# Powers of minus one half on ScalarE, one K copy by DMA, four more key tiles on VectorE

## The chip, the cores and the metric

The kernel runs on one core of one Trainium2 chip. It has five engines with a queue of instructions each: TensorE (PE, with its weight loads shown as PEld), VectorE (DVE), ScalarE (ACT), GpSimd (POOL) and SyncE (SP), which only issues DMAs here. Each engine takes its instructions strictly in the order in which the program lists them; where one waits on a semaphore, all behind it on that engine wait too. The metric is the device time of one execution in microseconds (us), median of several runs.

## The reference

The program is one transformer layer over 2048 tokens of 448 features, with weights and activations in bf16:

```python
x  = A_x
h  = x + attention(layernorm(x)) @ wo       # 16 query heads of 28, one shared key head and one shared value head
h2 = h + B(layernorm(h))
def B(x):                                   # mixture of depths
    r   = x @ w_r                           # one router score per token
    idx = argsort(-r)[:8]                   # the 8 best tokens
    y   = ((silu(x[idx] @ w_gate)) * (x[idx] @ w_up)) @ w_down
    return x + scatter_add(idx, y * sigmoid(r[idx]))
```

The layernorm is (x - mean) / sqrt(var + 1e-5), so each row of each of the two layernorms needs one power of minus one half. The attention is a full softmax, 16 heads times 2048 by 2048 scores; that is where the time goes.

## The kernel before, in words

**Tiles.** The 2048 tokens are 16 tiles of 128. A query block `b` is one such tile with all 16 heads, which lie as 4 strips of 4 heads; a strip has 32 rows of TensorE (28 features, one row that holds a constant, and padding) and 512 columns (4 heads by 128 queries). For each block and each key tile `j` the kernel makes 4 score products of 128 keys by 512 queries (line 834), turns them into exponentials, and multiplies these with the values of tile `j` (line 863), summed over all 16 key tiles in PSUM bank 7. One of the 32 value columns is a constant, so that the sum of exponentials comes out with the product.

**Two ways to an exponential.** There are 256 pairs of block and key tile. Most are done by ScalarE (`act_tile`, lines 872 to 897): two units of two strips each, 128 x 1024, one Exp per unit (line 888). The others are done by VectorE and GpSimd (`dve_tile`, lines 901 to 941): VectorE clamps the scaled scores of one strip to 16-bit integers, whose bits read as bf16 are a rough power of two (line 909, four per tile); GpSimd adds a constant to all four at once, twice, with a 64-bit integer add (line 920); the three versions are multiplied with three differently weighted copies of the values and so average out the roughness. A tile on VectorE therefore has 12 value products where a tile on ScalarE has 4. `_ND` lists how many of the 16 key tiles VectorE takes in each block: 83 in all, so ScalarE has 173 tiles, or 346 units.

**Two versions of K.** A score product of ScalarE's units is one over 64 rows of TensorE, in which the strip's neighbour is cancelled by zeros in K. So K is stored twice: version 0 has its data in rows 0 to 31 and 64 to 95 and zeros elsewhere, version 1 the other way round (`K[:, i % 2, ...]`, line 834). Both are written by VectorE out of the same PSUM bank (line 787), with per-partition factors in `kcol` that are zero where the version is to be zero. A unit of ScalarE has strips (0, 2), which read version 0, or (1, 3), which read version 1; the first comes first.

**The order of the work.** All instructions are first put into a graph with their dependencies, a planned duration and a priority (`G.op`). A planner (`_Flow.plan`) then walks through planned time, and at each step lists, on the engine that is free first, the ready instruction with the best priority; the result is the fixed order of each queue. Constants such as `_W`, `_LOOK`, `_WIN`, `_LATE` and `_HOLD` shift its choices; a DMA takes part with an issue of 400 ns on SP and a planned latency (`lat`, 2000 ns by default). An instruction with `lock=True` is planned so that it does not lie beside any instruction of GpSimd.

**Before the first block.** The tokens are normalized in groups of tiles (`group`, lines 725 to 800): 0, 1, (2, 3), (4, 5), (6, 7), (8 to 11), (12 to 15). For each: statistics (lines 730, 732), the power of minus one half, the normalized rows (lines 752 to 763), transposes on TensorE, the copy out of PSUM (line 777), the K product and its two writes (line 787), the V product and its write (line 796). In groups 0 to 2 the power is Exp(-0.5 Ln(var + eps)) on ScalarE (lines 735 and 737). From group 3 on it is `rsqrt` on VectorE (lines 713 to 723): a bit trick as first guess and three steps of Newton, with 14 small instructions per group in all. The groups 3 to 6 are worked through during block 0, since its key tiles need them one after the other. The large weights of the second half are loaded by SP at the same time (`weights`, lines 1040 to 1049): each piece of `wg_sb`, `wu_sb` and `wo_pad` waits on SP for an earlier piece to land.

**After each block.** The sum goes from PSUM to `Ot` (line 947), the softmax sums make a round trip through DRAM to be spread over the partitions (lines 951 to 955, four DMAs on SP), VectorE multiplies (`On`, line 956), TensorE projects and adds the residual, and VectorE works out the second layernorm and the router's score for the tile (`out_proj`, lines 962 to 1011): statistics (984, 985), `rsqrt` in its form with one product per step (986, 714 to 723, 8 instructions after line 986), `st3` (989), the router's product with its sum (993), the score `r_col` (996) and the output rows (1008). Block 15 has its own form on a short path (`last_rows`, lines 1013 to 1035), which uses Ln and Exp on ScalarE already.

**The end.** `stage1` (lines 1070 to 1106) finds the 8 best of tiles 0 to 13, gathers their rows and prepares them; `tail` (lines 1108 to 1246) finishes block 15, chooses the 8 best of all and runs the small network on them.

Of the kernel before, what the change touches and what calls it, by code (L numbers as in the profile page):

```python
# [237 lines left out]
MAGIC = 1597463007.0  # L238
# [269 lines left out]
def _fast(nc, G, sb, ps, psb, flag, scr, rows, A_x, A_wq, A_wk, A_wv, A_wo, B_w_r, B_w_gate, B_w_up, B_w_down, out):  # L508
# [178 lines left out]
    for r in range(2):  # L687
# [23 lines left out]
    kv_last = []  # L711

    def rsqrt(y, v, z, a, rd, wr, tmp, one=False):
        G.op(DV, lambda e: e.tensor_scalar(z.bitcast(I32), v.bitcast(I32), -0.5, MAGIC, ALU.mult, ALU.add), 62,
             reads=[rd], writes=[tmp])
        for n, c in enumerate((3.0, 12.0, 768.0)):
            if one:
                G.op(DV, lambda e: e.tensor_scalar(a, z, z, v, ALU.mult, ALU.mult), 62, reads=[tmp, rd], writes=[tmp])  # L718
            else:
                G.op(DV, lambda e: e.tensor_tensor(a, z, z, ALU.mult), 62, reads=[tmp], writes=[tmp])  # L720
                G.op(DV, lambda e: e.tensor_tensor(a, a, v, ALU.mult), 62, reads=[tmp, rd], writes=[tmp])
            G.op(DV, lambda e, c=c: e.scalar_tensor_tensor(z, a, -c, z, ALU.add, ALU.mult), 62, reads=[tmp], writes=[tmp])  # L722
        G.op(DV, lambda e: e.tensor_scalar(y, z, -1.0 / 8192.0, None, ALU.mult), 62, reads=[tmp], writes=[wr])

    def group(g):
# [3 lines left out]
        for t in tl_:  # L729
            G.op(DV, lambda e, t=t: e.bn_stats(bn6[:, t, :], x_sb[:, t, :]), 516, reads=[("x", t)], writes=[("bn6", t)],  # L730
                 after=[G.last_w[("xnT", 0)][0]] if t == 2 else [G.last_w[("nb", 3)][0]] if t in (4, 5) else (), prio=-3001 if g == 2 else None)
# [2 lines left out]
        if g < XA:
            G.op(AC, lambda e: e.activation(var[:, t0:t1], mv[:, t0:t1, 1], ACT.Ln, bias=ebias[:, 0:1]), 200,
                 reads=[("mv", t) for t in tl_] + ["ebias"], writes=[("var", g)])
            G.op(AC, lambda e: e.activation(rstd[:, t0:t1], var[:, t0:t1], ACT.Exp, scale=-0.5), 200, reads=[("var", g)],
                 writes=[("rstd", g)])
        else:
            G.op(DV, lambda e: e.tensor_scalar(var[:, t0:t1], mv[:, t0:t1, 1], EPS, None, ALU.add), 62,  # L740
                 reads=[("mv", t) for t in tl_], writes=[("var", g)])
            G.op(DV, lambda e: e.tensor_scalar(nmu[:, t0:t1], mv[:, t0:t1, 0], -1.0, None, ALU.mult), 62,
                 reads=[("mv", t) for t in tl_], writes=[("nmu", g)])
            rsqrt(rstd[:, t0:t1], var[:, t0:t1], nwt[:, t0:t1], nwt[:, NT + t0:NT + t1], ("var", g), ("rstd", g), ("nwt", g))
            G.op(DV, lambda e: e.tensor_tensor(nb[:, t0:t1], nmu[:, t0:t1], rstd[:, t0:t1], ALU.mult), 62,
                 reads=[("rstd", g), ("nmu", g)], writes=[("nb", t) for t in tl_])
        if 0 < g < XA:
# [38 lines left out]
        for r in range(2):  # L786
            G.op(DV, lambda e, r=r: e.tensor_scalar(K[:, r, sl], ps[:, uk.b[0], 0:w], kcol[:, r:r + 1],
                                                        kcol[:, 2 + r:3 + r], ALU.mult, ALU.add), 190 + w * 1.04,
                     reads=[uk.key, "k%d" % r, "kb%d" % r], writes=[("K", r, t) for t in tl_], free=uk)
# [87 lines left out]
    def spill(end):  # L877
        while strips:
            n = _UNIT[iu[0] % len(_UNIT)]
            if len(strips) < n or (end and len(strips) == 4 and n == 3):  # L880
                if not end:
# [7 lines left out]
                                                           scale=OCT), 63.3 + 426.5 * n,  # L889
# [55 lines left out]
    def evict(b):  # L945
# [11 lines left out]
                                           ALU.mult), 597, reads=[("Ot", rb), ("Rb", rb)], writes=[("On", rb)])  # L957
# [4 lines left out]
    def out_proj(t):  # L962
# [23 lines left out]
        G.op(DV, lambda e: e.tensor_scalar(st[:, t, 0:1], stf[:, 1:2], EPS, None, ALU.add), 62, reads=[("stf", t)],  # L986
# [833 lines left out]
```

## Time and profile before

| | |
|---|---|
| median of 3 runs | 378.29 us (378.02 to 378.76) |
| profiled execution, its own time | 377.05 us |
| span of the profiled execution, first to last instruction | 375.3 us |
| busy: PE, DVE, ACT, POOL | 336.3, 344.7, 335.5, 183.4 us |
| mean granted clock of TensorE | 0.964 of full speed |

A row of a group has the line, the engine, the operation, output and inputs with their shapes, the number of instructions, their busy time together in us, the mean of one in ns, and after the second bar the idle time of the engine just before them with what ended it. Busy time is the union of the instructions' times: where neighbours overlap it is less than number times mean. A row of the timeline has the start in us, the time in us of one or of several merged instructions, and in brackets the idle time before. L624 is the helper that makes a matmul and L636 the one that makes a DMA; there the tiles' names tell which one it is.

### The profile page before, as it was taken

How to read it: one execution, taken by the hardware profiler on the slowest of the kernel's cores; microseconds unless marked ns; L12 is line 12 of the kernel's file. 1: busy time of each engine (PE TensorE's matmuls, PEld its weight loads, DVE VectorE, ACT ScalarE, POOL GpSimd, SP SyncE). 2: the span in 40 equal slices, each digit the busy share in tenths (PEclk: the TensorE clock that was granted, in tenths of full speed). 3: DMA queues.
4: the chain of work that ended last, by engine and by line, in shares of the span. 5: the costliest groups of instructions: out<-in, count | busy, mean ns of one | idle time of the engine just before them, and what ended most of it. 6: DMA issues, size and time to landing. Idle time of an engine off the chain costs nothing.

```text
span 375.3 us, 8937 instructions
## 1 busy us (share of the span) xinstructions
PE 336.3 (90%) x3658; PEld 113.1 (30%) x3658; DVE 344.7 (92%) x859; ACT 335.5 (89%) x377; POOL 183.4 (49%) x197
## 2 busy tenths in 40 slices
PE   3967899999999999999988999999999999998965
PEld 2533332323232323222232323233232322222334
DVE  7999797999999999998989999999989999989884
ACT  5736999999999999989998999999999999998850
POOL 6010165754474647546445357655545656465311
PEclk9989999999999999977999999999999999998995
DMA  6662001001010001010010101010101610100010
GB/s 183 179 223 61 1 3 31 3 12 46 21 37 28 30 4 55 2 52 6 3 56 6 52 2 55 4 55 1 29 30 29 198 39 23 29 30 31 26 36 8
DMA packets 17975, 16.10 MB, mean 43 GB/s; under 512 B 6302, under 2 KB 15038, under 8 KB 17930
## 3 DMA queue, kind: packets, MB, share of 16 engines
q1 hardware_dynamic: 16426, 14.93, 12.8%
q8 instruction: 29, 0.48, 0.5%
q10 hardware_dynamic: 1392, 0.45, 0.5%
q14 instruction: 16, 0.13, 0.1%
q0 software_dynamic: 112, 0.12, 0.1%
HBM read 11.78 MB, written 3.71 MB: 41 GB/s over the span
## 4 chain that ended last, share of the span: by engine, by line
DVE 61%; PE 18%; ACT 11%; DMA 7%; issue 1%; POOL 0%; POOLq 0%; DVEq 0%
DVE Y L909 32%; ACT P L888 11%; PE ps L834 8%; PE ps L624 5%; PE ps L863 4%; DVE st L722 3%; DVE On L956 3%; DMA Rb<-l_scr 3%; DVE st L718 2%; DVE junk L993 2%; DVE of L1008 2%; DVE bn L984 2%; DMA l_scr<-Rc 2%; DMA x_sb<-in_A_x_dram 2%; DVE Ot L947 2%; DVE bn L730 1%
## 5 line engine op out<-in xcount | busy, mean ns | idle before, releaser
L888 ACT ACTIVATE P<-ps 128x1024 bf16<-128x1024 f32 x346 | 323.7, 1064 | 20.4 <-PE ps L834 18.6
L920 POOL INT64_ADD Yc<-Y x166 | 172.9, 1053 | 155.1 <-DVE Y L909 131.8
L909 DVE TENSOR_SCALAR Y<-ps 128x512 int16<-128x512 f32 x332 | 212.7, 679 | 13.0 <-PE ps L834 12.3
L834 PE MATMUL ps<-Q,K 32*128 32x512 bf16 (+1 forms) x1024 | 164.1, 395 | 13.2 <-DVE Y L909 5.0
L834 PEld LDWEIGHTS ps<-Q,K 32*128 32x128 bf16 (+1 forms) x1024 | 42.8, 92 | 142.6 <-ACT P L888 81.8
L863 PE MATMUL ps<-P,Vs 128*32 128x512 bf16 x692 | 65.0, 387 | 2.6 <-ACT P L888 2.2
L863 PE MATMUL ps<-Yc,Vs 128*32 128x512 bf16 x664 | 65.5, 396 | 0.5
L863 PE MATMUL ps<-Y,Vs 128*32 128x512 bf16 x332 | 33.9, 398 | 3.6 <-DVE Y L909 2.0
L863 PEld LDWEIGHTS ps<-Yc,Vs 128*32 128x32 bf16 x664 | 16.4, 94 | 29.4 <-issue 18.1
L863 PEld LDWEIGHTS ps<-P,Vs 128*32 128x32 bf16 x692 | 16.2, 95 | 21.8 <-issue 15.8
L624 PE MATMUL ps<-xnT,wqx 112*128 112x128 bf16 x256 | 21.1, 227 | 0.3 <-DVE Y L909 0.2
L624 PE MATMUL ps<-wo_pad,On 128*32 128x448 bf16 (+1 forms) x244 | 18.3, 357 | 1.6 <-DVE On L1124 1.4
L624 PEld LDWEIGHTS ps<-xnT,wqx 112*128 112x128 bf16 x256 | 15.2, 101 | 8.4 <-issue 5.8
L956 DVE TENSOR_TENSOR On<-Ot,Rb 128x512 bf16<-128x512 f32 x15 | 14.2, 944 | 2.0 <-DMA Rb<-l_scr 2.0
L863 PEld LDWEIGHTS ps<-Y,Vs 128*32 128x32 bf16 x332 | 8.6, 94 | 20.5 <-issue 8.8
L722 DVE SCALAR_TENSOR_TENSOR st<-st 128x1 f32<-128x1 f32 x45 | 13.2, 293 | 0.9
L772 PE MATMUL ps<-ident,of 128*112 128x128 bf16 x64 | 6.7, 259 | 8.0 <-DVE of L752 5.5
L718 DVE TENSOR_SCALAR st<-st 128x1 f32<-128x1 f32 x45 | 11.9, 265 | 0.4
L624 PE MATMUL ps<-x_sb,ident 128*32 128x448 bf16 (+1 forms) x82 | 10.4, 360 | 1.5 <-DVE On L956 1.0
L817 DVE TENSOR_SCALAR Q<-ps,qone 128x512 bf16<-128x512 f32 (+1 forms) x16 | 11.6, 723 | 0.0
L1008 DVE TENSOR_SCALAR of<-ps,st 128x448 bf16<-128x448 f32 x14 | 10.3, 735 | 0.0
L984 DVE BATCH_NORM_STATS2 bn<-ps 128x6 f32<-128x448 f32 x15 | 9.3, 623 | 0.9 <-PE ps L624 0.9
(170 smaller groups left out, 172.7 us busy)
## 6 DMA issues: line engine op xcount, KB each, us to landing
Rb<-l_scr SPq DMA_DIRECT2D x15, 256.0 KB
out_dram<-of SPq DMA_DIRECT2D x16, 112.0 KB, 2.2
n_rows<-of SPq DMA_DIRECT2D x14, 113.0 KB, 2.2
xnT<-in_B_w_down_dram SPq DMA_DIRECT2D x1, 1568.0 KB, 7.6
x_sb<-in_A_x_dram SPq DMA_DIRECT2D x3, 448.0 KB, 4.4
wg_sb<-in_B_w_gate_dram SPq DMA_DIRECT2D x1, 1344.0 KB, 8.8
wu_sb<-in_B_w_up_dram SPq DMA_DIRECT2D x1, 1344.0 KB, 6.2
wqx<-in_A_wq_dram ACTq DMA_DIRECT2D x1, 392.0 KB, 4.7
```

What stands on the lines that cost most here:

```text
L624: return lambda e: e.matmul(o() if callable(o) else o, lhsT=l, rhs=r, start=start, stop=stop)
L718: G.op(DV, lambda e: e.tensor_scalar(a, z, z, v, ALU.mult, ALU.mult), 62, reads=[tmp, rd], writes=[tmp])
L722: G.op(DV, lambda e, c=c: e.scalar_tensor_tensor(z, a, -c, z, ALU.add, ALU.mult), 62, reads=[tmp], writes=[tmp])
L817: G.op(DV, lambda e, c=c, src=src: e.tensor_scalar(Q[:, b % 3, c[0]:c[1], :], src(), qone[:, 0:1], None, ALU.add), 60 + n * 150, reads=[u. ...
L834: return e.matmul(ps[:, u.b[0] + q, :], lhsT=K[a:a + w, i % 2, j * 128:(j + 1) * 128], rhs=Q[a:a + w, b % 3, :, :].rearrange("p h n -> p ( ...
L863: return e.matmul(ps[32 * i:32 * i + 32, ACC, :], lhsT=Vs[:, v, j, :], rhs=src(i), start=info["first"] == o.idx, stop=info["last"] == o.idx)
L888: G.op(AC, lambda e, u=u, p=p, n=n: e.activation(P[:, p:p + n, :], ps[:, u.b[0]:u.b[0] + n, :], ACT.Exp, bias=EB, scale=OCT), 63.3 + 426.5 ...
L909: G.op(DV, lambda e, u=u, g0=g0: e.tensor_scalar(Y0[:, g0, :].bitcast(I16), ps[:, u.b[0], :], 0.0, TOP - STEP[-1], ALU.max, ALU.min), 599, ...
L920: G.op(PO, lambda e: e.int64_add(Yc[:, c, :, :].rearrange("p a b -> p (a b)").bitcast(I64), Y0[:, 4 * s:4 * s + 4, :].rearrange("p a b -> ...
L956: G.op(DV, lambda e: e.tensor_tensor(On[:, rb, :, :].rearrange("p h n -> p (h n)"), Ot[:, rb, :], Rb[:, rb, :], ALU.mult), 597, reads=[("O ...
L984: G.op(DV, lambda e: e.bn_stats(bn6[:, t, :], hp()), 545, reads=[u.key], writes=[("bn6", t)], free=u)
L1008: G.op(DV, lambda e: e.tensor_scalar(of[:, t, 0:D], hp(), st[:, t, 2:3], st[:, t, 3:4], ALU.mult, ALU.add), 652, reads=[u.key, ("st2", t), ...
```

## The change

Five things change, with a new set of the planner's constants.

- `rsqrt` is gone. Groups 3 to 6 and `out_proj` of blocks 0 to 14 use Ln and Exp on ScalarE. The normalized rows then take mean and power directly, so that `nmu` and `nb` are no longer needed there.
- `r_col` is gone. The router's score of a tile is worked out in one step for tiles 0 to 13 (`rp`) and one for tile 14.
- From group 1 on, VectorE writes K version 0 only. Version 1 is copied from it by two DMAs per group on SP (32 partitions each), into a tensor that GpSimd has zeroed at the start.
- `On`, the normalized rows of the groups and the step for `rp` are planned with `lock=True`: not beside GpSimd's integer adds.
- `_ND` gives VectorE 87 key tiles instead of 83, and ScalarE 169 instead of 173; block 0 has 3 on VectorE instead of 1. The planned length of an Exp goes from 63.3 + 853 to 50 + 853 ns, that of an integer add from 1130 to 1060 ns.

```diff
-_ND = (1, 8, 5, 4, 6, 6, 6, 3, 6, 5, 7, 6, 4, 7, 4, 5)
+_ND = (3, 7, 4, 6, 7, 6, 5, 5, 6, 6, 6, 3, 7, 7, 4, 5)
-_SHIFT = 1130
+_SHIFT = 1060
...
+    G.op(PO, lambda e: e.memset(K[:, 1, 128:S], 0.0), 1750, writes=["K1"])
...
-    def rsqrt(y, v, z, a, rd, wr, tmp, one=False):
...
-        if g < XA:
-            G.op(AC, lambda e: e.activation(var[:, t0:t1], mv[:, t0:t1, 1], ACT.Ln, bias=ebias[:, 0:1]), 200,
...
-            rsqrt(rstd[:, t0:t1], var[:, t0:t1], nwt[:, t0:t1], nwt[:, NT + t0:NT + t1], ("var", g), ("rstd", g), ("nwt", g))
...
+        G.op(AC, lambda e: e.activation(var[:, t0:t1], mv[:, t0:t1, 1], ACT.Ln, bias=ebias[:, 0:1]), 200,
+             reads=[("mv", t) for t in tl_] + ["ebias"], writes=[("var", g)])
+        G.op(AC, lambda e: e.activation(rstd[:, t0:t1], var[:, t0:t1], ACT.Exp, scale=-0.5), 200, reads=[("var", g)],
+             writes=[("rstd", g)])
...
+                G.op(DV, lambda e, t=t: e.tensor_scalar(of[:, t, 0:D], x_sb[:, t, :], mv[:, t, 0:1], rstd[:, t:t + 1],
+                                                        ALU.subtract, ALU.mult), 300,
+                     reads=[("x", t), ("mv", t), ("rstd", g)], writes=[("of", t)], lock=True)
...
-        for r in range(2):
+        for r in range(2 if g == 0 else 1):
             G.op(DV, lambda e, r=r: e.tensor_scalar(K[:, r, sl], ps[:, uk.b[0], 0:w], kcol[:, r:r + 1],
...
+        if g > 0:
+            for r in range(2):
+                dma(K[64 * r + 32:64 * r + 64, 1, sl], K[64 * r:64 * r + 32, 0, sl], [("K", 1, t, r) for t in tl_],
+                    reads=["K1"] + [("K", 0, t) for t in tl_], lat=2100.0)
...
-                                                           scale=OCT), 63.3 + 426.5 * n,
+                                                           scale=OCT), 50.0 + 426.5 * n,
...
-                                           ALU.mult), 597, reads=[("Ot", rb), ("Rb", rb)], writes=[("On", rb)])
+                                           ALU.mult), 599, reads=[("Ot", rb), ("Rb", rb)], writes=[("On", rb)], lock=True)
...
-        G.op(DV, lambda e: e.tensor_scalar(st[:, t, 0:1], stf[:, 1:2], EPS, None, ALU.add), 62, reads=[("stf", t)],
+        G.op(AC, lambda e: e.activation(st[:, t, 0:1], stf[:, 1:2], ACT.Ln, bias=ebias[:, 0:1]), 200, reads=[("stf", t), "ebias"],
              writes=[("st0", t)])
-        rsqrt(st[:, t, 1:2], st[:, t, 0:1], st[:, t, 6:7], st[:, t, 7:8], ("st0", t), ("st1", t), ("stn", t), one=True)
+        G.op(AC, lambda e: e.activation(st[:, t, 1:2], st[:, t, 0:1], ACT.Exp, scale=-0.5), 200, reads=[("st0", t)],
+             writes=[("st1", t)])
...
-        G.op(DV, lambda e: e.tensor_scalar(r_col[:, t:t + 1], st[:, t, 3:4], sw[:, 0:1], st[:, t, 4:5],
-                                           ALU.mult, ALU.add), 182,
-             reads=[("st3", t), "sw", ("st4", t)], writes=[("r", t)])
...
-        G.op(DV, lambda e: e.tensor_copy(rp[:, 0:N1], r_col[:, 0:N1]), 62, reads=[("r", t) for t in range(N1)],
-             writes=["rp1"])
+        G.op(DV, lambda e: e.scalar_tensor_tensor(rp[:, 0:N1], st[:, 0:N1, 3], sw[:, 0:1], st[:, 0:N1, 4], ALU.mult, ALU.add),
+             100, reads=["sw"] + [(k, t) for t in range(N1) for k in ("st3", "st4")], writes=["rp1"], lock=True)
```

More of the change, by code (lines that the diff above doesn't have):

```diff
@@ L709, in _fast @@
                  after=[G.last_w["wq_pad"][0]])
-    kv_last = []
-    def rsqrt(y, v, z, a, rd, wr, tmp, one=False):
[L714 to L723, printed above, removed]
+    kv_last, late = [], range(1, NT)
     def group(g):
@@ L730, in group @@
             G.op(DV, lambda e, t=t: e.bn_stats(bn6[:, t, :], x_sb[:, t, :]), 516, reads=[("x", t)], writes=[("bn6", t)],
[L731 removed]
+                 after=[G.last_w[("xnT", 0)][0]] if t == 2 else [G.last_w[("of", 3)][0]] if t in (4, 5) else (), prio=-3001 if g == 2 else None)
             G.op(DV, lambda e, t=t: e.bn_aggr(mv[:, t, :], bn6[:, t, :]), 89, reads=[("bn6", t)], writes=[("mv", t)],
                  prio=-3001 if g == 2 else None)
[L734 to L747 removed]
+        G.op(AC, lambda e: e.activation(var[:, t0:t1], mv[:, t0:t1, 1], ACT.Ln, bias=ebias[:, 0:1]), 200,
+             reads=[("mv", t) for t in tl_] + ["ebias"], writes=[("var", g)])
+        G.op(AC, lambda e: e.activation(rstd[:, t0:t1], var[:, t0:t1], ACT.Exp, scale=-0.5), 200, reads=[("var", g)],
+             writes=[("rstd", g)])
+        if 0 < g < XA and any(t < 3 for t in tl_):
             G.op(DV, lambda e: e.scalar_tensor_tensor(nb[:, t0:t1], mv[:, t0:t1, 0], -1.0, rstd[:, t0:t1], ALU.mult, ALU.mult), 70,
@@ L844, in scores @@
         o = G.op(PE, [part(q, *p) for q, p in enumerate(parts)] if parts else strip, 231,
-                 reads=[("Q", b_ % 3) for b_, j_ in need] + [("K", r, j_) for b_, j_ in need for r in range(2)] +
+                 reads=[("Q", b_ % 3) for b_, j_ in need] + [("K", r, j_) for b_, j_ in need for r in range(2) if j_ not in late or r == 0] +
+                 [("K", 1, j_, r) for b_, j_ in need for r in range(2) if j_ in late] +
                  [("Qa", 0)] * (need[0][0] == 0), writes=[("U", kind, b, j, k)], prio=(-2950.0 if kind == "A" and b == j == 0 else -100.0 + key) + W[kind], take=u,
@@ L1747, in bass_sequential_preLN__grouped_kv_mqa__moe_arch_mod__prompt_kernel @@
         s_join = es.enter_context(nc.semaphore("m_join"))
-        dsems = [es.enter_context(nc.semaphore("md%d" % i)) for i in range(120)]
+        dsems = [es.enter_context(nc.semaphore("md%d" % i)) for i in range(134)]
         ring = [es.enter_context(nc.semaphore("mr%d" % i)) for i in range(_NY)]
```

23 lines of the change are left out of this document (9 added, 14 removed).

## The prediction

> **What bounds the kernel now.** I read the page's busy times first, then ScalarE's own timeline, then the windows and the waits. The page and its slices:
>
> ```profile
> span 375.3 us, 8937 instructions
> PE 336.3 (90%) x3658; PEld 113.1 (30%) x3658; DVE 344.7 (92%) x859; ACT 335.5 (89%) x377; POOL 183.4 (49%) x197
> ...
> PEclk9989999999999999977999999999999999998995
> ```
>
> Three engines are near 90%, so the shares alone decide nothing. ScalarE's timeline, Exps merged where the gaps are small, says more:
>
> ```profile
> 11.06 2.15 ACT L888 ACTIVATE P<-ps 128x1024 bf16<-128x1024 f32 x2 [0.23 <-PE ps L834]
> 13.87 1.94 ACT L888 ACTIVATE P<-ps 128x1024 bf16<-128x1024 f32 x2 [0.66 <-PE ps L834]
> 16.83 3.77 ACT L888 ACTIVATE P<-ps 128x1024 bf16<-128x1024 f32 x4 [1.02 <-PE ps L834]
> 26.34 7.51 ACT L888 ACTIVATE P<-ps 128x1024 bf16<-128x1024 f32 x8 [5.74 <-PE ps L834]
> 37.68 71.27 ACT L888 ACTIVATE P<-ps 128x1024 bf16<-128x1024 f32 x77 [3.83 <-PE ps L834]
> ...
> 347.16 7.74 ACT L888 ACTIVATE P<-ps 128x1024 bf16<-128x1024 f32 x8 [0.49 <-PE ps L834]
> ```
>
> and who holds TensorE up, with the group of the Exps and three windows (PE, PEld, DVE, ACT, POOL busy, then the granted clock):
>
> ```profile
> PEld ps L834 <- ACT P L888: 81.8, 206, 0.8
> ```
>
> ```profile
> L888 ACT ACTIVATE P<-ps 128x1024 bf16<-128x1024 f32 x346 | 323.7, 1064 | 20.4 <-PE ps L834 18.6
> ```
>
> ```profile
> 160.00:180.00 20.00, 18.98 (x164) 4.86 (x160) 18.10 (x35) 17.88 (x19) 10.26 (x10) 0.74 0.08 27
> 180.00:200.00 20.00, 17.49 (x188) 5.49 (x192) 18.22 (x40) 18.08 (x21) 9.57 (x10) 1.00 0.09 28
> ...
> 220.00:240.00 20.00, 19.17 (x213) 5.88 (x213) 19.86 (x43) 19.96 (x23) 13.38 (x14) 1.00 0.09 28
> ```
>
> One Exp lasts 1064 ns, but neighbours overlap: in the run of four at 16.83 us the first three take (3.77 - 1.06) / 3 = 0.903 us each. That is ScalarE's pace when nothing is missing. With it the span splits into: 11.06 us before the first Exp; 26.6 us up to 37.68, in which only 16 Exps run (14.4 us), so 12.2 lost; 317.2 us up to 354.90 for the other 330 Exps (298.0 us), so 19.2 lost; and a tail of 20.4 us. From 37.68 on ScalarE is the bound: TensorE waits 81.8 us in 206 places for it to give a bank back. VectorE, at 19.86 of 20 in the same window, is a second one close behind, and in the opening it is the first one: the gaps of 5.74 and 3.83 us are waits for K, which VectorE's groups make. So a change that frees VectorE pays only where VectorE makes ScalarE wait, that is in the opening, in part of the 19.2 us, and at the end; and whatever is put on ScalarE is paid in full.
>
> **Fewer Exps.** Four tiles leave ScalarE, 8 units by 0.903: **-7.2 us**. In their place VectorE gets 16 clamps, GpSimd 8 adds and TensorE 32 more value products:
>
> ```profile
> L909 DVE TENSOR_SCALAR Y<-ps 128x512 int16<-128x512 f32 x332 | 212.7, 679 | 13.0 <-PE ps L834 12.3
> L920 POOL INT64_ADD Yc<-Y x166 | 172.9, 1053 | 155.1 <-DVE Y L909 131.8
> L863 PE MATMUL ps<-Yc,Vs 128*32 128x512 bf16 x664 | 65.5, 396 | 0.5
> ```
>
> That is 16 x 212.7 / 332 = 10.3 us of VectorE, 8.4 of GpSimd (49% busy) and 32 x 65.5 / 664 = 3.2 of TensorE, which its waits for ScalarE cover. If VectorE had no room the 10.3 us would cost about as much as the Exps save, but it gets room:
>
> ```profile
> L956 DVE TENSOR_TENSOR On<-Ot,Rb 128x512 bf16<-128x512 f32 x15 | 14.2, 944 | 2.0 <-DMA Rb<-l_scr 2.0
> L722 DVE SCALAR_TENSOR_TENSOR st<-st 128x1 f32<-128x1 f32 x45 | 13.2, 293 | 0.9
> L718 DVE TENSOR_SCALAR st<-st 128x1 f32<-128x1 f32 x45 | 11.9, 265 | 0.4
> ...
> L996 DVE TENSOR_SCALAR r_col<-st,sw 128x1 f32<-128x1 f32 x15 | 4.0, 265 | 0.0
> ...
> L986 DVE TENSOR_SCALAR st<-of 128x1 f32<-128x1 f32 x15 | 2.2, 145 | 0.1
> L714 DVE TENSOR_SCALAR st<-st 128x1 int32<-128x1 int32 x15 | 2.2, 145 | 0.1
> L723 DVE TENSOR_SCALAR st<-st 128x1 f32<-128x1 f32 x15 | 2.1, 142 | 0.2
> ...
> L721 DVE TENSOR_TENSOR nwt<-nwt,var 128x4 f32<-128x4 f32 x6 | 0.9, 156 | 0.0
> ```
>
> ```profile
> L787 DVE TENSOR_SCALAR K<-ps,kcol 128x256 bf16<-128x256 f32 (+2 forms) x14 | 7.5, 572 | 1.8 <-PE ps L624 1.8
> ```
>
> The powers of the 15 blocks take 13.2 + 11.9 + 2.2 + 2.2 + 2.1 = 31.6 us of VectorE, the scores 4.0; the powers of four groups are 56 small instructions of about 0.156, 8.7 us; of K's 14 writes 6 go, 6 x 0.572 = 3.4 us. Together 47.7 us out and 10.3 in: VectorE's 344.7 comes to about 307, 82% of the span.
>
> `On` takes 0.944 us on average where a clamp of the same 512 columns takes 0.64 at its pace. Planned apart from GpSimd it should gain up to 15 x 0.3 = 4.5 us of VectorE, more room, while POOL, busy half the time, loses under a microsecond at each; I count nothing for it. The Trainium skill (SBUF — State Buffer, SBUF: two separate sides) says why: a VectorE instruction with two SBUF inputs and a GpSimd one that reads SBUF hold a shared port pair by turns, the later one blocked for the whole instruction. The trace agrees as far as `On`, with two SBUF inputs, is the slow one; by the rule the gain stays on VectorE and the sum is the same.
>
> **Ln and Exp on ScalarE.** The groups before 3 have run the pair:
>
> ```profile
> L735 ACT ACTIVATE var<-mv,ebias 128x1 f32<-128x1 f32 x2 | 0.6, 278 | 0.0
> ...
> L737 ACT ACTIVATE rstd<-var 128x1 f32<-128x1 f32 x2 | 0.4, 203 | 0.1
> ```
>
> A pair costs at most 0.278 + 0.203 = 0.48 us; if both overlap their neighbours as an Exp does (1.064 - 0.903 = 0.16), 0.16. I take the middle, 0.32, since an Exp of the scores can stand between the two in one place and not in another. 14 pairs fall on the bound stretch: **+4.5** (2.2 to 6.7). The pairs of the four groups fall into the opening, where ScalarE idles, and cost nothing as long as it does; without that cover they cost 1.3.
>
> Both are also new waits on ScalarE's queue: Ln waits for line 985 on VectorE, and behind it stand the next Exps, and behind these TensorE. I take no cost, because VectorE will have room and the statistics can be done well ahead; the price if not is a rival below.
>
> **The opening.** VectorE is relieved of the 8.7 and some 3 us of K writes, about 12 of its work before 37.68 us, and the loss that hangs on it is 5.74 + 3.83. Against this, version 1 of K comes later by a DMA, and on SP it stands among the weights:
>
> ```profile
> 13.21 0.37 SPq L636 DMA_DIRECT2D w_rb<-in_B_w_r_dram  x1
> 13.62 0.43 SPq L636 DMA_DIRECT2D wg_sb<-in_B_w_gate_dram  x1
> 14.88 0.35 SPq L636 DMA_DIRECT2D wo_pad<-in_A_wo_dram  x1
> 22.48 0.59 SPq L636 DMA_DIRECT2D wg_sb<-in_B_w_gate_dram  x1
> 23.11 0.57 SPq L636 DMA_DIRECT2D wu_sb<-in_B_w_up_dram  x1
> 23.73 0.48 SPq L636 DMA_DIRECT2D wo_pad<-in_A_wo_dram  x1
> 29.33 0.48 SPq L636 DMA_DIRECT2D wu_sb<-in_B_w_up_dram  x1
> ```
>
> ```profile
> w_rb<-in_B_w_r_dram SPq DMA_DIRECT2D x1, 112.0 KB, 4.7
> x_sb<-in_A_x_dram SPq DMA_DIRECT2D x2, 112.0 KB, 2.4
> Lall<-l_scr SPq DMA_DIRECT2D x15, 8.0 KB, 1.6
> ```
>
> SP stands still from 15.2 to 22.48 and from 24.2 to 29.33, until a weight has landed; the planner counts 2 us for each of these loads and so will list the copies of groups 2 to 4 near or behind them. Copies that are free of the queue land 1.6 us after K and the opening gains up to 8 of the 9.6 us. Copies of groups 3 and 4 behind the wait at 29.33 land at about 31.4; the 8 Exps of tiles 4 to 7, on which 26.34 to 33.85 was spent, then end near 39, and the opening loses 2. Between -8 and +2 I take **-3**, since some copies will stand behind a weight, and VectorE, no longer busy, lets what follows be ready at once. GpSimd's zeroing of K lies before the values are needed.
>
> The Trainium skill (DMA: Bandwidth & Descriptors, Queues, rings and completion order) adds that each DMA engine takes the descriptors of one queue in ring order. The trace agrees: 112 KB right ahead of the big load took 4.7 us to land, where 112 KB took 2.4 earlier. By this rule even a copy issued in time lands only with the weight ahead of it, and the opening would gain nothing; that is the first rival.
>
> **The long stretch.** Of the 19.2 us lost, about 6 lie between 160 and 200 (4.0 of idle time in the two windows and slower Exps), where the clock was 0.74 for 20 us; freeing VectorE does nothing for that. The other 13 are many small delays of TensorE, some by VectorE and GpSimd. Bounds: -10, nearly all of these, and +3, if the new order has more of them; I take **-4**.
>
> **The tail.** The last blocks' shuffle stands behind the power of tile 14 and a wait for a DMA:
>
> ```profile
> 356.53 0.15 DVE L1091 TENSOR_SCALAR ti<-cidx 112x1 int32<-112x1 int32 x1 [0.60 <-DMA cidx<-gidx]
> ...
> 357.04 0.44 DVE L1115 STREAM_SHUFFLE Ot<-ps 128x256 f32<-128x256 f32 x1
> ```
>
> The last Exp ended at 354.90 and its products within half a microsecond, so 1.6 us are there to gain; if the DMA's wait still stands ahead, 0.5. I take **-1** (-1.6 to +0.5).
>
> **The sum.** -7.2 + 4.5 - 3 - 4 - 1 = -10.7, so a span of 364.6. The profiled execution had 377.05 - 375.3 = 1.75 outside its span and was 1.24 under the median: 364.6 + 1.75 + 1.24 = **367.6 us**.
>
> **The rivals.**
>
> *Copies behind weights.* The opening loses 2 instead of gaining 3; the rest as above: -5.7, **372.6**. For it: SP's two long waits. Against it: tiles 0 to 3 need little of it, and part of this delay stands in VectorE's place.
>
> *VectorE was the hidden bound.* If most of the small losses and nearly all of the opening were its doing: -7.2 + 3.4 - 8 - 10 - 1.5 = -23.3, **355.0**. For it: 19.86 of 20 in the window at 220. Against it: every gap names TensorE, and ScalarE had 19.96 there.
>
> *Slower: ScalarE waits for statistics.* At each `out_proj` Ln stands in ScalarE's queue, and its input hangs on the DMA round trip of `Rb`, `On`, five products, and lines 984 and 985. Any lateness d against the plan, which VectorE or PE now bear alone, is paid on ScalarE 15 times. It cancels the gain from d = 10.7 / 15 = 0.71 us on; with 1.1, somewhat over a late statistics instruction, it is +5.8, **384**. The row of `On` speaks against it: only 2.0 us of waiting for `Rb` in 15 blocks.
>
> *No change.* Pairs at their upper price (+6.7) eat the 7.2, and opening, stretch and tail come out even: **377.8**.
>
> **How the numbers follow.** Forecast 0.50, with a range of its own of 362 to 372; copies behind weights 0.19; hidden bound 0.12; ScalarE waits 0.12; no change 0.07. A measurement tells 0.2%, 0.76 us, from nothing. The first three are faster: 0.81; same 0.07; slower 0.12. The range runs from 359, which cuts off over half of the hidden bound, to 378.5, which leaves out the slower case; all bounds at once (353.6 and 383.3 in span) are not needed for 8 in 10.
>
> **What would show it.** The Exps' row has x338 at a pace of 0.903; lines 718 and 722 are gone, VectorE's busy time is near 307 and ScalarE's within 3 us of 335.5; a row of Ln has x15 with little idle time before it; the eighth Exp ends before 22 us and the 16th before 36. Idle time of ScalarE before Ln of over 8 us, or an opening whose 16th Exp ends after 38, would prove the forecast wrong.

## The result and the profile after

The changed kernel takes 366.09 us (median of 4 runs, 365.21 to 367.52) where the kernel before took 378.52 in the same session (378.02 to 381.39): a ratio of 0.966, with an interval of 0.960 to 0.972. The profiled execution took 365.21 us with a span of 363.2. The total is 1.5 us below the forecast, but two of its terms were far off, in opposite directions. The page after, with the slices of the granted clock and the chain of waits by engine (followed back from the last instruction, at each step to what released it):

```profile
span 363.2 us, 8869 instructions
...
PE 327.5 (90%) x3690; PEld 109.8 (30%) x3690; DVE 318.0 (88%) x663; ACT 327.8 (90%) x407; POOL 194.3 (54%) x206
...
PEclk9976899999999999999999999999999999999995
...
ACT 77%; PE 10%; DMA 6%; DVE 4%; issue 1%; POOL 0%; POOLq 0%; ACTq 0%; SPq 0%; DVEq 0%
```

Its groups of the scores' Exps, the clamps and `On` (line 870 is line 888 of before, 891 is 909, 938 is 956; 815 further down is 834, and 968 and 970 are Ln and the power's Exp of `out_proj`):

```profile
L870 ACT ACTIVATE P<-ps 128x1024 bf16<-128x1024 f32 x338 | 314.4, 1209 | 13.6 <-PE ps L815 13.5
L891 DVE TENSOR_SCALAR Y<-ps 128x512 int16<-128x512 f32 x348 | 220.3, 681 | 15.5 <-PE ps L815 15.0
L938 DVE TENSOR_TENSOR On<-Ot,Rb 128x512 bf16<-128x512 f32 x15 | 10.5, 701 | 0.7 <-DMA Rb<-l_scr 0.7
```

The mean of one Exp, 1209 ns for 1064, is not its cost: in the run of 25 below, at 82.24 us, each takes 23.16 / 25 = 0.93 us, since neighbours overlap more. ScalarE's timeline, the opening and the first pair in the stretch:

```profile
11.10 2.15 ACT L870 ACTIVATE P<-ps 128x1024 bf16<-128x1024 f32 x2 [0.23 <-PE ps L815]
16.82 0.48 ACT L720 ACTIVATE var<-mv,ebias 128x2 f32<-128x2 f32 x2 [3.58 <-DVE mv L718]
...
24.18 1.94 ACT L870 ACTIVATE P<-ps 128x1024 bf16<-128x1024 f32 x2 [4.81 <-PE ps L815]
...
34.46 1.94 ACT L870 ACTIVATE P<-ps 128x1024 bf16<-128x1024 f32 x2 [5.91 <-PE ps L815]
...
43.51 37.82 ACT L870 ACTIVATE P<-ps 128x1024 bf16<-128x1024 f32 x41 [0.34 <-PE ps L815]
81.05 0.45 ACT L968 ACTIVATE st<-of,ebias 128x1 f32<-128x1 f32 x1
81.25 1.16 ACT L870 ACTIVATE P<-ps 128x1024 bf16<-128x1024 f32 x1
82.15 0.34 ACT L970 ACTIVATE st<-st 128x1 f32<-128x1 f32 x1
82.24 23.16 ACT L870 ACTIVATE P<-ps 128x1024 bf16<-128x1024 f32 x25
...
334.44 9.46 ACT L870 ACTIVATE P<-ps 128x1024 bf16<-128x1024 f32 x10
```

The span splits as in the prediction. Before 43.51 us only 15 Exps ran, at 0.903 us 13.5 of the 32.4 us since 11.10: 18.9 lost. From there to 343.90, 300.4 us hold 323 Exps (291.7) and the pairs: between Ln and the next Exp lie 0.20 us, between the power's Exp and the next 0.09, so 14 pairs cost 4.1, and 4.6 us are lost. The tail is 363.2 - 343.9 = 19.3.

| part of the span | predicted, us | measured, us |
|---|---|---|
| start | 0 | 0.0 |
| 8 Exps fewer | -7.2 | -7.2 |
| pairs on ScalarE | +4.5 | +4.1 |
| opening | -3 (-8 to +2) | +6.7 (18.9 for 12.2) |
| long stretch | -4 (-10 to +3) | -14.6 (4.6 for 19.2) |
| tail | -1 | -1.1 |
| sum | -10.7 | -12.1 |

**Where the opening went.** SP's timeline after, the waits of TensorE's weight loads (PEld) and products (PE) for the copies (us in total, times, longest), and the time to landing of all twelve:

```profile
12.22 1.26 SPq L633 DMA_DIRECT2D K<-K  x2
...
14.60 0.76 SPq L633 DMA_DIRECT2D wg_sb<-in_B_w_gate_dram  x1
16.49 1.15 SPq L633 DMA_DIRECT2D K<-K  x2
...
23.05 0.54 SPq L633 DMA_DIRECT2D wg_sb<-in_B_w_gate_dram  x1
23.64 0.59 SPq L633 DMA_DIRECT2D wu_sb<-in_B_w_up_dram  x1
...
30.07 0.49 SPq L633 DMA_DIRECT2D wu_sb<-in_B_w_up_dram  x1
30.61 1.23 SPq L633 DMA_DIRECT2D K<-K  x2
...
32.49 14.64 SPq L633 DMA_DIRECT2D K<-K  x6
```

```profile
PEld ps L815 <- DMA K<-K: 9.0, 2, 5.2
PE ps L815 <- DMA K<-K: 8.0, 2, 4.3
```

```profile
DMA to landing us min/median/max: 1.7/2.0/6.7
```

The copies of two groups pay. Group 2's, issued at 16.49 right behind the first big load, land up to 6.7 us later instead of 1.7: ScalarE's gap of 4.81. Group 3's are not issued before 30.61, since SP stands until 30.07 for a piece of `wu_sb` that waits for the one before it: the gap of 5.91. These gaps are 10.7 of the 18.9 us. A third, of 3.58, stands before the Ln of groups 2 and 3, which waits for VectorE's statistics with the next Exps behind it. Ln is not what makes these late: the products of the third Exp run at 16.69, where before ran them at 13.22. In the version without copies (below) the third Exp starts at 14.18 for 17.45 here, and with the late weights at 16.51, so some 2 to 3 us go with the copies even where no weight is in their way; that this is their planned landing is likely and not shown.

**Where the stretch came from.** The page of before had a line that the prediction did not use, and its waits another:

```profile
DVE 61%; PE 18%; ACT 11%; DMA 7%; issue 1%; POOL 0%; POOLq 0%; DVEq 0%
```

```profile
PEld ps L834 <- DVE Y L909: 21.0, 56, 1.5
...
PE ps L834 <- DVE Y L909: 5.0, 13, 1.2
```

and after:

```profile
PEld ps L815 <- ACT P L870: 112.7, 264, 0.8
...
PEld ps L815 <- DVE Y L891: 5.5, 22, 0.5
```

The weight loads of the score products waited 21.0 us for a late clamp to give a bank back, and now 5.5; their waits for ScalarE grew from 81.8 to 112.7, and the chain of waits passed from VectorE (61%) to ScalarE (77%). A weight load waits while earlier products still run, so these are not losses one for one: ahead of the products themselves TensorE stood idle behind clamps for 5.0 us. The reading is that before, VectorE's lateness reached ScalarE through TensorE, whose products stand in a fixed order. The granted clock is a rival, for in the stretch it was 1.00 after and lower before (PE, PEld, DVE, ACT, POOL busy, then the clock; before first):

```profile
45.04:354.89 309.85, 291.67 (x3120) 87.56 (x3120) 292.03 (x639) 301.07 (x323) 172.86 (x166) 0.98 0.10 31
```

```profile
51.82:343.89 292.07, 279.61 (x3151) 82.50 (x3150) 272.94 (x515) 291.72 (x343) 182.90 (x175) 1.00 0.11 33
```

Experiments were needed to tell VectorE's room, a better plan and the clock apart.

### The profile page after: what moved, and what is told of

Read it like the earlier page. It is cut to its first block, busy times and chain, and to the rows that moved or that the text cites. A ratio compares the mean times of both kernels' runs of the same rounds, so it can differ in the third digit from the quotient of the medians.

```text
span 363.2 us, 8869 instructions
## 1 busy us (share of the span) xinstructions
PE 327.5 (90%) x3690; PEld 109.8 (30%) x3690; DVE 318.0 (88%) x663; ACT 327.8 (90%) x407; POOL 194.3 (54%) x206
## 4 chain that ended last, share of the span: by engine, by line
ACT 77%; PE 10%; DMA 6%; DVE 4%; issue 1%; POOL 0%; POOLq 0%; ACTq 0%; SPq 0%; DVEq 0%
ACT P L870 75%; PE ps L621 5%; PE ps L815 3%; DMA K<-K 2%; DMA Rb<-l_scr 1%; PE ps L845 1%; DMA wqx<-in_A_wq_dram 1%; PE ps L749 1%; DMA l_scr<-Rc 1%; DVE Y L891 1%; DVE of L738 1%; ACT st L968 1%; DVE K L764 1%; ACT st L970 0%; ACT wqx L703 0%
## 5 line engine op out<-in xcount | busy, mean ns | idle before, releaser
L870 ACT ACTIVATE P<-ps 128x1024 bf16<-128x1024 f32 x338 | 314.4, 1209 | 13.6 <-PE ps L815 13.5
L902 POOL INT64_ADD Yc<-Y x174 | 182.2, 1059 | 139.3 <-DVE Y L891 126.0
L891 DVE TENSOR_SCALAR Y<-ps 128x512 int16<-128x512 f32 x348 | 220.3, 681 | 15.5 <-PE ps L815 15.0
L815 PE MATMUL ps<-Q,K 32*128 32x512 bf16 (+1 forms) x1024 | 151.0, 389 | 19.3 <-ACT P L870 10.0
L815 PEld LDWEIGHTS ps<-Q,K 32*128 32x128 bf16 (+1 forms) x1024 | 38.8, 91 | 148.0 <-ACT P L870 112.7
L845 PE MATMUL ps<-Yc,Vs 128*32 128x512 bf16 x696 | 62.3, 384 | 0.0
L845 PE MATMUL ps<-P,Vs 128*32 128x512 bf16 x676 | 60.8, 392 | 1.1 <-DVE Ot L929 0.9
L845 PEld LDWEIGHTS ps<-P,Vs 128*32 128x32 bf16 x676 | 14.8, 94 | 31.0 <-issue 25.5
L621 PE MATMUL ps<-xnT,wqx 112*128 112x128 bf16 x256 | 21.7, 232 | 0.1
L621 PE MATMUL ps<-wo_pad,On 128*32 128x448 bf16 (+1 forms) x244 | 19.2, 357 | 0.0
L621 PE MATMUL ps<-x_sb,ident 128*32 128x448 bf16 (+1 forms) x82 | 10.4, 360 | 1.5 <-DVE Y L891 1.4
L938 DVE TENSOR_TENSOR On<-Ot,Rb 128x512 bf16<-128x512 f32 x15 | 10.5, 701 | 0.7 <-DMA Rb<-l_scr 0.7
L764 DVE TENSOR_SCALAR K<-ps,kcol 128x128 bf16<-128x128 f32 (+2 forms) x8 | 4.4, 550 | 7.5 <-PE ps L621 7.4
L754 DVE COPY xnT<-ps 112x1024 bf16<-112x1024 bf16 (+1 forms) x9 | 5.6, 629 | 5.5 <-PE ps L749 5.3
```

The source lines that it names most:

```text
L621: return lambda e: e.matmul(o() if callable(o) else o, lhsT=l, rhs=r, start=start, stop=stop)
L815: return e.matmul(ps[:, u.b[0] + q, :], lhsT=K[a:a + w, i % 2, j * 128:(j + 1) * 128], rhs=Q[a:a + w, b % 3, :, :].rearrange("p h n -> p ( ...
L845: return e.matmul(ps[32 * i:32 * i + 32, ACC, :], lhsT=Vs[:, v, j, :], rhs=src(i), start=info["first"] == o.idx, stop=info["last"] == o.idx)
L870: G.op(AC, lambda e, u=u, p=p, n=n: e.activation(P[:, p:p + n, :], ps[:, u.b[0]:u.b[0] + n, :], ACT.Exp, bias=EB, scale=OCT), 50.0 + 426.5 ...
L891: G.op(DV, lambda e, u=u, g0=g0: e.tensor_scalar(Y0[:, g0, :].bitcast(I16), ps[:, u.b[0], :], 0.0, TOP - STEP[-1], ALU.max, ALU.min), 599, ...
L902: G.op(PO, lambda e: e.int64_add(Yc[:, c, :, :].rearrange("p a b -> p (a b)").bitcast(I64), Y0[:, 4 * s:4 * s + 4, :].rearrange("p a b -> ...
```

## The experiments

Times are given as the ratio to the kernel before, run on the same chip, since chips differ (its medians went from 375.85 to 378.52). "Against the change" is the difference to 0.966 times 378.5 us; the intervals of both leave it uncertain by 2 to 5 us, so losses are also read from each profile: *opening*, from the first Exp to the 25th beyond 0.903 us each, and *stretch*, from there to the last Exp beyond 0.903 each, pairs included. On this scale before has 12.3 and 19.1, the change 19.0 and 8.5. The losses are of one profiled run each. Where the order is frozen, the planner's order of the changed kernel is kept and only the added instructions are put in, and nothing reads what they write; everywhere else the order is planned anew.

**The large weights after the last copy of K.**

```diff
-        big = [xd[-1]]
-        for w_, A_, nm in ((wg_sb, B_w_gate, "wg"), (wu_sb, B_w_up, "wu")):
...
+    def late_weights():
+        G.prio = 0.3
+        big = [G.last_w[("K", 1, NT - 1, 1)][0]]
+        for w_, A_, nm in ((wg_sb, B_w_gate, "wg"), (wu_sb, B_w_up, "wu")):
...
```

`late_weights` is called at 0.75 of block 0.

> The changed kernel with the four loads of wg_sb and wu_sb issued only after the last K copy. Theory Q (K copies stand behind weights in SP's queue and in the DMA rings, and this costs the opening 6.7 us against before instead of gaining 3): TensorE's 8.0 us of waiting for K copies shrink to under 2, the 16th Exp ends before 36 us instead of about 44, and the time falls from 366.1 to 355 to 359. Rival (the copy's own 2 us and TensorE's order make the opening slow, whatever lies in the queue): 366 within 1 us.

Measured: 353.81 us, ratio 0.9422 (0.9406 to 0.9439), 9.0 against the change and the fastest version of this study. Its span, SP's timeline, ScalarE's timeline and the landing of the copies:

```profile
span 351.4 us, 8869 instructions
```

```profile
22.97 12.57 SPq L633 DMA_DIRECT2D K<-K  x6
36.83 6.44 SPq L633 DMA_DIRECT2D wg_sb<-in_B_w_gate_dram  x2
```

```profile
31.47 2.15 ACT L870 ACTIVATE P<-ps 128x1024 bf16<-128x1024 f32 x2 [0.37 <-PE ps L815]
33.88 10.43 ACT L870 ACTIVATE P<-ps 128x1024 bf16<-128x1024 f32 x11 [0.27 <-PE ps L815]
```

```profile
DMA to landing us min/median/max: 1.7/1.8/3.1
```

The 16th Exp ends at 32.5 instead of 44.5, the opening loses 7.7 instead of 19.0, and the stretch 8.8 for 8.5. That the copies were late behind the weights is shown.

**Both versions of K by VectorE, no copies.**

```diff
-        for r in range(2 if g == 0 else 1):
+        for r in range(2):
...
-        if g > 0:
-            for r in range(2):
-                dma(K[64 * r + 32:64 * r + 64, 1, sl], K[64 * r:64 * r + 32, 0, sl], ...
```

> The changed kernel with both versions of K written by VectorE again in all groups, no copies, no zeroing by GpSimd. Theory Q: the opening is freed as in the run with late weights, but for 3.4 us more of VectorE in it: 357 to 362, and the 16th Exp ends before 38 us. Rival (not the copies but Ln and Exp on ScalarE's queue, or the new order, hold the opening up): 365 to 368.

Measured: ratio 0.9483 (0.9467 to 0.9499), 6.7 against the change; opening 9.5, stretch 10.0. So the copies, as placed, cost time. With the weights out of their way they beat VectorE's writes, by 0.9422 to 0.9483, each in its own plan.

**The copies issued by GpSimd.** `eng=PO` is added to the two copies of each group; the weights stay.

> The changed kernel with the twelve K copies issued by GpSimd instead of SP; the weights stay on SP as they were. Theory Q1 (the copies were late by standing in SP's queue, and as a queue of their own they share the DMA engines by turns): all copies land within 3 us, the opening loses about 8 us as with the late weights, ratio to before 0.940 to 0.948. Theory Q2 (the data of the weights hold up any copy): TensorE still waits some 4 us for the copies of group 2, ratio 0.952 to 0.962.

Measured: ratio 0.9798 (0.9694 to 0.9903), 5.2 slower than the change. The opening fell by 4.1 to 14.9, but the new plan loses 14.1 in the stretch (5.6 more) and 1.9 in the tail, so the total fits neither theory. The copies, in the view of DMA issues (KB of each, median us from issue to landing):

```profile
K<-K POOLq DMA_DIRECT2D x4, 32.0 KB, 1.8
K<-K POOLq DMA_DIRECT2D x6, 16.0 KB, 5.1
```

On one queue the large late copies land in 1.8 us and the small early ones, beside the weights, in 5.1. Another queue removes SP's waiting, not the delay beside the weights. The Trainium skill (DMA: Bandwidth & Descriptors, Queues, rings and completion order) has each DMA engine go round its queues packet by packet. By that rule one expects a copy from a second queue to get in early between a load's packets; a median 3.3 us above that of the late copies is more than this leads one to expect, and the measurement decides. What in the early copies' surroundings holds them up is not shown.

**The planner is told when the weights land.**

```diff
-            big.append(dma(w_[:, 0:3, :], ..., [nm], after=big[-1:]))
-            dma(w_[64:128, 3, :], A_[384:448], [nm + "3"], after=big[-1:])
+            big.append(dma(w_[:, 0:3, :], ..., [nm], after=big[-1:], lat={"wg": 8400.0, "wu": 6400.0}[nm]))
+            dma(w_[64:128, 3, :], A_[384:448], [nm + "3"], after=big[-1:], lat=3400.0)
```

> The changed kernel with one thing told to the planner: the loads of wg_sb and wu_sb land after 8.4, 6.4 and 3.4 us (as in its trace) and not after 2. SP's order then has the copies of groups 3 and 4 ahead of the second load of wg_sb; the copies of group 2 still go right behind the first. Theory Q (waiting in SP's queue and waiting behind data are two costs of about 4 us): the wait of 4.3 us at about 34 us goes, that of 3.7 at about 23.5 stays; 3 to 6 us below the changed kernel, ratio 0.950 to 0.958. Rival (one cause only, the data in flight): less than 1.5 us below.

Measured: 360.22 us, ratio 0.9551 (0.9477 to 0.9624), 4.1 against the change, as the theory of two costs had it; opening 14.8, stretch 8.4. What is left is the delay of the data of group 2's copies:

```profile
PE ps L815 <- DMA K<-K: 5.5, 2, 4.6
```

The last two experiments, each in a plan of its own, agree on some 4 us of the opening for SP's in-order wait; loading the weights after the copies takes away 7.1 more.

**VectorE's time back, in heaps.** Three statistics of unused output follow `st2` in each of blocks 0 to 13, order frozen.

```diff
+        if t < N1:
+            G.extra[s2.idx] = [lambda e, k=k: e.bn_stats(dum[:, t, k, :], x_sb[:, 0, :]) for k in range(3)]
```

> The order of the changed kernel, untouched, with three statistics instructions of 448 columns (0.6 us each) put on VectorE behind the step st2 of blocks 0 to 13, into a tile that nothing reads: 42 x 0.6 = 25 us of VectorE, somewhat less than the powers and scores that the change took off it (35.6). Theory R (it was VectorE's room that cut the loss of the long stretch from 19.2 to 4.6 us): most of the 14.6 comes back, 374 to 380. Rival N (the room is not needed; a better order or the clock cut the loss): below 369.

**The same amount, spread.** 43 of them, one behind the last clamp of every second tile, order frozen.

```diff
+            if k == 3 and m % 2:
+                G.extra[cl.idx] = [lambda e, m=m: e.bn_stats(dum[:, m, :], x_sb[:, 0, :])]
```

> The order of the changed kernel, untouched, with one statistics instruction of 0.6 us behind the last clamp of every second key tile of VectorE, 43 in all, 26 us: as much as in the run with three in a row per block, but spread. Theory R as a matter of the sum (VectorE has no room left, each microsecond on it is paid): 20 to 34 us above the changed kernel, as with the heaps. Rival B (it was the heap of 1.8 us that made TensorE and ScalarE stand; spread load is taken up by what room there is): less than 10 us above.

Measured: the heaps 1.0454 (1.0407 to 1.0501), 30 us over the change, more than either theory had; spread 1.0133 (1.0067 to 1.0199), 17.9 over it, between the theories. The heaps' Exps, and the additions:

```profile
L874 ACT ACTIVATE P<-ps 128x1024 bf16<-128x1024 f32 x338 | 320.0, 1072 | 41.5 <-PE ps L819 40.7
...
L986 DVE BATCH_NORM_STATS2 dum<-x_sb 128x6 f32<-128x448 bf16 x42 | 23.4, 612 | 0.0
```

the Exps and the wait behind clamps of the spread ones:

```profile
L874 ACT ACTIVATE P<-ps 128x1024 bf16<-128x1024 f32 x338 | 318.8, 1042 | 24.7 <-PE ps L819 23.4
```

```profile
PEld ps L819 <- DVE Y L895: 24.3, 67, 0.9
```

VectorE's busy time rose by 22 us in both (339.7 and 340.0 for 318.0), to less than it had before the change. So a microsecond of VectorE costs 17.9 / 22.0 = 0.8 us when spread and 30 / 21.7 = 1.4 in heaps of 1.8 us, although VectorE is busy for under 90% of the span. With the spread ones the wait behind clamps goes from 5.5 back to 24.3, before's 21.0.

But the 1.4 is not VectorE's alone, for the heaps' clock was much lower (0.904 to 0.933 in its runs, 0.959 to 0.974 for the change; in the stretch of the profile 0.92, with the spread ones 0.98). What a low clock costs can be estimated from runs of one kernel: before took 374.47 us at a mean of 0.977 and 379.54 at 0.957 on one chip, 5.1 us for 0.020 x 375 = 7.5 us of missing clock, or 0.7 for one. At that rate 0.08 x 326 us of the heaps' stretch is some 18 of the 34 us that it lost more than the change, and 0.02 x 311 is some 4 of the 18.8 of the spread ones. By this estimate both doses cost about 0.7 us per us of VectorE, and heaps are not shown to be dearer; whether they bring the low clock about is open. The heaps' profile is of its longest run (398.17 us, the others 390.81 to 394.52), so its 42.5 us in the stretch overstate.

**Time on ScalarE.** Four Ln of one column in each of blocks 0 to 13, order frozen.

```diff
+            G.extra[ex.idx] = [lambda e, k=k: e.activation(dum[:, t, k:k + 1], mv[:, 0, 1:2], ACT.Ln, bias=ebias[:, 0:1]) for k in range(4)]
```

> The order of the changed kernel, untouched, with four more Ln of one column each on ScalarE behind the Exp of the power in blocks 0 to 13, 56 in all, into a tile that nothing reads. Theory S (ScalarE is the bound and pays all that is put on it): 56 x 0.1 to 0.19 = +5.6 to +10.6, 371.7 to 376.7. Rival (ScalarE has room in the long stretch): under +2, below 368.

Measured: ratio 1.000 (0.9964 to 1.0037), 12.9 over the change, more than the theory's 10.6; the profiled span is 9.0 longer, which lies within it, 8.9 of that in the stretch. 56 instructions: 0.16 us each by the profile, the pace among neighbours, though one lasts 0.42:

```profile
L977 ACT ACTIVATE dum<-mv,ebias 128x1 f32<-128x1 f32 x56 | 13.6, 422 | 0.0
```

ScalarE's time is paid in full: its busy time rose by 9.3 us (337.1 for 327.8), and in the stretch it is busy for all of 301.0 us, in the change for 291.7 of 292.1 (the clock is 1.00 in both), before for 301.1 of 309.9. TensorE, busy for 90% of the span too, was given no such dose; what a microsecond on it costs is not shown.

**Before, with only the blocks' powers moved.** In the kernel before, lines 986 and 988 become Ln and Exp on ScalarE, nothing else.

> The kernel before with one part of the change alone: Ln and Exp on ScalarE for the powers of blocks 0 to 14; its own constants, its 83 tiles, its K, no locks. Theory R: 4 us for the pairs, 7 to 14 off the loss of the stretch, so 3 to 10 us faster than before (ratio 0.973 to 0.992) with an opening like before's. Rival N (it takes the new constants or the locks): no faster than before, up to 4 us slower.

Measured: ratio 0.9898 (0.9846 to 0.9949), 3.9 us faster than before. Opening 12.7, stretch 14.5, of which 4.1 are pairs: like for like 10.4 for 19.1. VectorE's busy time is 320.4, 24.3 less. The clock of the stretch is 0.98 as in before, so these 8.7 us are not the clock's. The weight loads' wait behind clamps is 15.2 for 21.0.

**The change, with the blocks' powers back on VectorE.** `rsqrt` returns for the 15 blocks; 87 tiles stay.

> The changed kernel with the powers of blocks 0 to 14 by the bit trick and three Newton steps on VectorE again, planned anew. Theory R (VectorE's room cut the loss of the long stretch): VectorE has some 32 us more, ScalarE 4 less; the loss of the stretch, 8.5 us with the pairs, comes to 20 or more, and the time is 8 to 20 us above the changed kernel's. Rival N (the room is not needed, ScalarE is the bound): 0 to 4 us below the changed kernel's.

Measured: ratio 1.0171 (1.0084 to 1.0259), 19.3 over the change and slower than before. The stretch loses 23.2 without any pair, 4.4 with the powers on ScalarE, at a clock of 0.97; the tail is 4.9 longer. VectorE is at 342.3:

```profile
L879 ACT ACTIVATE P<-ps 128x1024 bf16<-128x1024 f32 x338 | 314.6, 1125 | 28.1 <-PE ps L824 20.0 <-PE ps L854 7.2
```

More tiles on VectorE without the room for them lose more than the eight Exps give.

**The change with 83 tiles.** `_ND` of before, everything else as changed.

> The changed kernel with the list of key tiles of the kernel before: 83 on VectorE, 1 in block 0, planned anew. ScalarE gets 8 Exps back (+7.2 us), VectorE loses 16 clamps (-10.3). Theory S, that of the prediction (ScalarE alone is the bound of the long stretch): 5 to 8 us above the changed kernel. Theory B (VectorE's time is paid too, at about 0.7 us for one, as the run with the spread load says): +7.2 - 7.2, within 2 us of the changed kernel.

Measured: ratio 0.9968 (0.9925 to 1.0011), 11.7 over the change by the ratio, 10.0 by the profiled span: eight Exps 7.2, opening 0.6, stretch 1.0, tail 1.4. VectorE is at 309.9, 8 us less, and ScalarE gets nothing for it. That goes beyond the theory that had 5 to 8 and speaks, as far as one new plan can, against the one that had at most 2.

**Without the locks.** `, lock=True` is dropped in three places; then the same with the weights after the copies.

> The changed kernel planned without the three lock marks (On, the normalized rows, the step for rp); nothing else, but the whole order is planned anew. Theory L (keeping VectorE's two-input instructions apart from GpSimd's adds earns time): On's mean goes from 701 ns back to about 940, VectorE has 4 us more, and as VectorE's time is paid in this kernel the time is 3 to 6 us higher than the changed kernel's. Rival (off the path): within 1.5 us of the changed kernel, whatever On does.

> The kernel with the late weights, planned without the three lock marks: the same question as in the run without locks, on a plan whose opening is clean. Theory L (the locks earn time in the long stretch): 3 to 6 us above the kernel with the late weights, ratio to before 0.950 to 0.958, On near 930 ns, the loss of the stretch up from 8.8 to 11 or more. Rival (the 6 us in the other run were the luck of a new plan): within 1.5 us, 0.938 to 0.946.

Measured: 0.9828 (0.9754 to 0.9903), 6.4 over the change, the stretch losing 12.0 for 8.5; and 0.9492 (0.9426 to 0.9559) for 0.9422 (0.9406 to 0.9439), 2.7 over the late weights and between the two theories. The second's profile loses 15.6 in the stretch for 8.8, but it is of the longest of four runs (361.69 us at a clock of 0.966, the others 356.84 to 360.15 at 0.985 or 0.986). `On` in the second:

```profile
L938 DVE TENSOR_TENSOR On<-Ot,Rb 128x512 bf16<-128x512 f32 x15 | 14.6, 972 | 1.6 <-DMA Rb<-l_scr 1.5
```

Planned without the locks `On` takes 972 ns on average (931 in the first), with them 701. The sign is the same twice, though the intervals of the second pair overlap; the size is not settled.

The stretch loss by VectorE's busy time, of all but the run with more on ScalarE, with the clock of that stretch:

| kernel | VectorE busy, us | clock | stretch loss, us (pairs in it) |
|---|---|---|---|
| change, 83 tiles | 309.9 | 0.99 | 9.5 (4.1) |
| change, weights last | 317.1 | 0.99 | 8.8 (4.1) |
| change, landing told | 317.5 | 1.00 | 8.4 (4.1) |
| the change | 318.0 | 1.00 | 8.5 (4.1) |
| change, copies from GpSimd | 319.7 | 0.99 | 14.1 (4.1) |
| change, no locks | 320.1 | 0.99 | 12.0 (4.1) |
| before, powers on ScalarE | 320.4 | 0.98 | 14.5 (4.1) |
| weights last, no locks | 320.8 | 0.98 | 15.6 (4.1) |
| change, K by VectorE | 322.0 | 1.00 | 10.0 (4.1) |
| change, heaps | 339.7 | 0.92 | 42.5 (4.1) |
| change, spread additions | 340.0 | 0.98 | 27.3 (4.1) |
| change, powers on VectorE | 342.3 | 0.97 | 23.2 (0) |
| before | 344.7 | 0.98 | 19.1 (0) |

Four kernels at 318 us and below lose 8.4 to 9.5, so nothing more comes back there, as far as these show. Around 320 us the loss runs from 10.0 to 15.6 at nearly the same busy time, so plan and clock count for several us. A price of VectorE's time can be read only where the order is frozen.

## Why the prediction was right in total, and wrong in two steps

**Fewer Exps: right.** x338 at 0.903, -7.2, and 83 tiles give it back.

**Ln and Exp: right.** 0.29 us a pair for my 0.32, and the dose has 0.16 for one instruction. The Trainium skill (ScalarE: Activation LUTs, What ACT_TABLE_LOAD costs) has 280 and 186 ns for a short one with and without a pointer as bias and an overlap of 93; the estimate from it, 280 + 186 - 2 x 93 or 0.28 us, agrees with 0.29. In the stretch no wait of ScalarE for statistics showed: the row of Ln has 0.3 us of idle time in 15 instances, so the slower rival fell, as the row of `On` had suggested. The 3.58 us before the first Ln of the opening cost next to nothing, as the products behind it were late as well.

```profile
L968 ACT ACTIVATE st<-of,ebias 128x1 f32<-128x1 f32 x15 | 6.4, 425 | 0.3 <-DVE of L967 0.3
```

**The opening: wrong, sign and size.** The step that failed is "some copies will stand behind a weight", taken at -3 with +2 as the worst. Both delays that I had described, SP's wait and the landing behind a load, were paid one after the other by different groups, and VectorE's relief bought nothing while K was missing: +6.7. I had priced only the copies of groups 3 and 4, at 1.6 us from issue, and none for group 2, whose copies took 6.7. The 112 KB in 4.7 us that I had shown were of a transfer issued ahead of the big load, and so no evidence for a delay behind one. By the test that I set, a 16th Exp after 38 us, this step fell: it ended at 44.5. The first rival was what happened here, worse than its +2.

**The long stretch: wrong in size.** The step that failed is "From 37.68 on ScalarE is the bound", with TensorE's 81.8 us of waiting for it and ScalarE's 19.96 of 20 us in one window as the witnesses. The 81.8 were waits of weight loads beside running products, and VectorE's line of 21.0 us in 56 places and the chain's 61% went unread. ScalarE was full in that window, but it lost 19.2 us over the whole stretch, and a good part of these was VectorE's doing through TensorE. The stretch brought -14.6 where I took -4 and had -10 as the bound; in this term it was the second rival, beyond its price. Moving the blocks' powers alone brings 8.7 of it at the same clock of 0.98. The other 6 lie between the clock, the locks (3.5 by one profile), the 87 tiles and the plan, and are not told apart: I counted the clock's dip as there to stay, and it was absent after, which by the rate estimated above is some 0.7 x 0.02 x 310 = 4 us, with no cause shown.

**VectorE's busy time: wrong.** I expected 307 and it is 318.0. The clamps grew by 7.6 us and `On` gave 3.7, better than assumed; the 47.7 us of small instructions gave less. Before, moving powers with a summed 31.6 us (15 blocks) took only 24.3 off the busy time, and part of that is `On` at 782 ns. Small instructions overlap their neighbours, so the sum of their times overstates what goes with them. ScalarE's busy time is 7.7 below, not within 3: the Exps of the scores have 9.3 less, and all else on ScalarE only 1.6 more, as the pairs largely lie within their neighbours' times.

**The tail: right**, -1.1.

**The sum** was right by luck: an opening 9.7 us worse and a stretch 10.6 us better than forecast cancelled. Each rival had been priced alone; that two could come together was not considered. The 353.6 and 383.3 that I called spans are times of an execution.

## What to carry to other kernels

Before work moves to a DMA, look up what the issuing queue stands for at that time and what big load is in flight: here a copy of 1.8 us cost up to 6.7, and loading the weights later made a gain of 3.4% one of 5.8%. When two engines are near 90%, read the chain of waits and who makes TensorE wait before naming one the bound, and test it by adding some work to each in an otherwise frozen order: ScalarE cost 1 us per us and VectorE about 0.8, though taking another 8 us off VectorE brought nothing. Look at the granted clock of the same stretch before putting a loss down to an engine. Give the planner the landing times that the trace shows, not a default.

## What the hardware showed that I had not expected

- A 16 KB copy from on-chip memory to on-chip memory lands 1.7 to 1.8 us after issue alone, 6.7 behind a load of 1344 KB on the same queue, and 5.1 (median of six) beside one on another.
- The same 22 us of VectorE cost 17.9 us when spread and 30 in heaps, the latter at a clock of 0.92 for 0.98 in the stretch.
- A kernel's time follows TensorE's mean granted clock from run to run: the kernel before, on one chip, took 374.47 us at 0.977 and 379.54 at 0.957, the change 365.23 at 0.974 and 367.52 at 0.960. In the change's profile the low clock (0.66 between 20 and 40 us) lies where TensorE waits for K, in before's (0.74 between 160 and 180) where it is 95% busy. With the weights last and no locks it is 0.66 between 40 and 60 us, with TensorE busy for 19.77 of 20. What sets it is open. The window of after (PE, PEld, DVE, ACT, POOL busy, then the clock):

```profile
20.00:40.00 20.00, 12.18 (x78) 5.10 (x78) 9.39 (x26) 8.31 (x12) 0.79 (x2) 0.66 0.39 130
```
